# First batch rearranged: k transposed from f32, the DFT's sums and residual in PSUM, a written order of work, and new turns for the later stages

## The chip, the core and the metric

The kernel runs on one core of one Trainium2 chip. A core has a matrix engine (PE, with its weight loads shown apart as PEld), a vector engine (DVE), a scalar engine (ACT), GpSimd (POOL) and a sync engine (SP) that here only issues DMAs. PE writes to PSUM, of which this kernel uses eight banks; all POOL operations here read and write SBUF. Times are device microseconds of one execution; the number that counts is the median of several.

## What is computed

Four batches, eight heads, 768 positions, 64 columns per head. First a decayed linear attention, then an FFT over the sequence and over the 512 model columns, of which the real part is kept, then a normalised feed-forward layer:

```python
for t in range(S):
    state = gamma * state + einsum('bhd,bhe->bhde', k[:, :, t], v[:, :, t])
    y[:, :, t] = scale * einsum('bhd,bhde->bhe', q[:, :, t], state)
x = y.transpose(0, 2, 1, 3).reshape(B, S, H * D)
u = x + real(fft(fft(x, axis=1), axis=2))
un = (u - mean(u)) / sqrt(var(u) + 1e-6)
out = u + maximum(un @ w_ch1, 0.0) @ w_ch2        # 512 -> 2048 -> 512
```

## The kernel before

**Attention.** The sequence is cut into six chunks of 128 rows and the heads into four pairs. For each pair: q, k, v are loaded in f32 (`load_unit`, 384 KB each, on SP), cast to f16 on POOL (`q0_unit`, `k0_unit`, which scales k by a decay per row, `v0_unit`). PE transposes q and k with an identity (`t0_unit`, line 433), ACT copies the results out (`te_unit`, lines 441 and 444). PE forms the scores of each chunk (`am_unit`, wkA, line 458), DVE masks and scales them into atm (`ae_unit`, line 465). PE forms k'v of each chunk (`kv0_unit`, wkK, line 480), and one DVE scan runs the state through the chunks (`sc_unit`, line 489). The output y is atm v plus q times the state (`yi_unit`, `yx_unit`, lines 504 and 520); ACT scales it into x (`x0_unit`, line 533). Heads 4 to 7 lie mirrored in the second half of x. Pairs come in the order 0, 1, 3, 2.

**DFT.** Symmetry halves it twice. DVE folds x over the sequence (`fold_s`, tile xab, line 673), then over the columns (`fold_d`, tile eo, line 683). PE multiplies by cosine and sine tables (`s1_unit`, ps, line 730), ACT and DVE copy the result out as g (lines 737 and 739). The edge columns go a way of their own (`g0_a`, `g0_b`, `g0_c`). The second DFT (`s2_unit`, psum pq, lines 843 and 847) gives 128 rows of the mixed result: its two parts P and Q are joined by an ACT copy qn (line 855) and two DVE operations into u (lines 856 and 858). In the first batch's rows 0 to 383 (row blocks kb 0 to 2) half of x is put into pq first (`px_unit`), the mean comes from x (`xmean_unit`, `mean_unit`), and `norm_unit` writes un = mean - u (line 879); elsewhere POOL adds x (lines 864 and 866) and DVE takes the statistics. PE transposes un (`unT_unit`, line 914).

**Feed-forward.** `h_unit` and, for the first three row blocks, `h0_unit` (psh, lines 930 and 947) form relu(un w1), evicted by ACT or DVE into ht16; `ch_unit` (psc, line 973) multiplies by w2, DVE adds u, SP stores. The weights are cast while they are loaded, by eight DMAs on POOL's queue (`w1_unit`, `w2_unit`, lines 987 and 994).

**Order.** The engines run their instructions in program order. For the first batch the order is a hand-written list in `first_units`, and `pin` makes each engine keep it. Fillers, matmuls of zeros into a PSUM tile that nobody reads (`filler`, line 145), stand between its steps. All after that is a set of streams: each stream is a list of units with a start and an end in units of one batch's feed-forward work, `emit` sorts all units by that due time, and the attention and DFT of batch b + 1 so come to lie between the feed-forward matmuls ("majors") of batch b. The loads of the second batch wait for the seventh weight DMA and for a feed-forward matmul. From the third batch on, q, k and un are transposed by DMAs on SP.

**PSUM.** Five banks (ps_g) go round; two more (ps_y) and one for fillers (ps_w) serve the first batch alone and are given back, and three (ps_pm) for the feed-forward products take their place.

Of the kernel before, what the change touches and what calls it, by code (L numbers as in the profile page):

```python
# [18 lines left out]
P = 128  # L19
# [12 lines left out]
FB = 1  # L32
NPE = 2
ACT_ROWS = ((2, 5, 6, 7, 8, 9, 10, 14), (0, 3, 6, 7, 9, 10, 11, 12, 14, 15), (2, 4, 5, 6, 7, 8, 10, 14))
# [3 lines left out]
def kernel(  # L38
# [32 lines left out]
    first = ExitStack()  # L71
    ps_y = first.enter_context(tc.tile_pool(name="ps_y", bufs=2, space=PSUM))
    ps_w = first.enter_context(tc.tile_pool(name="ps_w", bufs=1, space=PSUM))
    ps_pm = None
# [65 lines left out]
    wps = ps_w.tile([P, DM], f32, tag="w", name="wps")  # L140

    def filler(n):
        def run():
            for _ in range(n):
                nc.tensor.matmul(wps, wz[:, 0:P], wz, start=True, stop=True)  # L145
        return run
# [5 lines left out]
    def load_unit(b, i, after=None):  # L152
        def run():
            h0 = 2 * PAIR_ORDER[i]
            for name, src in srcs.items():
# [3 lines left out]
                dma = nc.sync.dma_start(t, src[b, h0:h0 + 2].rearrange(rows, p=P))  # L159
# [21 lines left out]
    gexp = const.tile([P, 2, H], f32, tag="gexp")  # L181
    gq8, gkd = gexp[:, 0], gexp[:, 1]
    ident16 = const.tile([P, P], f16, tag="ident16")
    tmp = up.tile([P, NCH, DM], f32, tag="u32", name="tmp")
# [3 lines left out]
    rs = [tmp[:, 2 + n] if n < 4 else tmp2[:, n - 4] for n in range(10)]  # L188
    icoln = const.tile([P, 5], f32, tag="icoln")
# [8 lines left out]
    for h in range(H):  # L198
# [6 lines left out]
                            op0=ALU.mult)  # L205
    nc.scalar.activation(gexp, gexp, AF.Exp, bias=0.0, scale=1.0)
# [4 lines left out]
    make_identity(nc, ident16)  # L211
    nc.gpsimd.affine_select(out=maskf, in_=maskf, compare_op=ALU.is_ge, fill=0.0, base=0,
# [15 lines left out]

    def late_consts():
        with tc.issue_after(lb[0]["una"].ins):  # L230
            for h in range(H):
                nc.scalar.activation(maskp[:, h // 2, h % 2], maskf, AF.Copy, bias=0.0,
                                     scale=float(gam[h] ** (-P)))
# [59 lines left out]
    def csn_unit(c):  # L293
        def run():
            nc.scalar.activation(csn[:, c, :], rs[2 * c + 1][:, 0:384], AF.Sin, bias=hpi,
                                 scale=-float(2.0 * np.pi / S))
        return run
# [46 lines left out]
    def half_ids():  # L344
        nc.gpsimd.tensor_scalar(out=hid, in0=ident16, scalar1=0.5, scalar2=1.0, op0=ALU.mult,
                                op1=ALU.mult)
        nc.gpsimd.tensor_scalar(out=nhid, in0=ident16, scalar1=-0.5, scalar2=1.0, op0=ALU.mult,
                                op1=ALU.mult)

# [3 lines left out]
    at, q16_of, kd_of, v16_of, last_cast = {}, {}, {}, {}, {}  # L353
# [42 lines left out]
    def k0_unit(i):  # L396
        def run():
            h0 = 2 * PAIR_ORDER[i]
            k32 = in_of.pop(("k", 0, i))
            kd = kd_of[0, i] = kp.tile([P, NCH, 2, D], f16, tag="kd16", name="kd16")  # L400
            nc.gpsimd.tensor_scalar(out=kd[:, :, 0, :], in0=k32[:, 0], scalar1=gkd[:, h0:h0 + 1],
                                    scalar2=1.0, op0=ALU.mult, op1=ALU.mult)
            if i < 3:
                nc.gpsimd.tensor_scalar(out=kd[:, :, 1, :], in0=k32[:, 1],
                                        scalar1=gkd[:, h0 + 1:h0 + 2], scalar2=1.0,
                                        op0=ALU.mult, op1=ALU.mult)
            else:
                nc.scalar.activation(kd[:, :, 1, :], k32[:, 1], AF.Copy, bias=0.0,
                                     scale=gkd[:, h0 + 1:h0 + 2])
        return run  # L410

    def v0_unit(i):
        def run():
            v32 = in_of.pop(("v", 0, i)).rearrange("p h c d -> p c h d")
            v16 = v16_of[0, i] = vp.tile([P, NCH, 2, D], f16, tag="v16", name="v16")
            n = NCH if i < 3 else 3
            last_cast[0, i] = nc.gpsimd.tensor_scalar(
                out=v16[:, 0:n], in0=v32[:, 0:n], scalar1=1.0, scalar2=1.0, op0=ALU.mult,
                op1=ALU.mult)
            if n < NCH:  # L420
                nc.vector.tensor_copy(v16[:, n:], v32[:, n:])
        return run

    def t0_unit(i, part):
        def run():
            if part == 0:
                at[0, i] = dict(kT=tp.tile([P, NCH, P], f16, tag="kT", name="kT"),
                                qT=qts[i % 2][:, 0])
            src = (q16_of, kd_of)[part][0, i]
            tq = at[0, i]["tq", part] = ps_g.tile([P, NCH, P], f16, tag="g", name="tq",  # L430
                                                  padded_shape=[P, 8, P])
            for c in range(NCH):
                nc.tensor.transpose(tq[:, c, :], src[:, c].rearrange("p a b -> p (a b)"), ident16)
        return run

    def te_unit(i, part):
        def run():
            st = at[0, i]
            tq = st["tq", part]
            if part == 0:  # L440
                nc.scalar.copy(st["qT"].rearrange("p c t -> p (c t)").rearrange(
                    "p (t c) -> p t c", c=NCH), tq.rearrange("p c t -> p t c"))
            else:
                nc.scalar.copy(st["kT"], tq)
        return run

    def am_unit(i, half):
        def run():
            st = at[0, i]
            if half == 0:  # L450
                st["atm"] = ap_.tile([P, NCH, 2, P], f16, tag="atm", name="atm")
# [10 lines left out]
    def ae_unit(i, half, h2):  # L462
        def run():
# [3 lines left out]
                scalar=float(gam[2 * PAIR_ORDER[i] + h2] ** (-P)),  # L467
                in1=maskf.unsqueeze(1).to_broadcast([P, 3, P]), op0=ALU.mult, op1=ALU.mult)
        return run
# [25 lines left out]
    def yi_unit(i, h2):  # L495
        def run():
            st = at[0, i]
            first = i < 3
            if first:
                st["y", h2] = ps_y.tile([P, NCH, D], f32, tag="y", name="wkY",  # L500
                                        padded_shape=[P, 8, D])
# [7 lines left out]
    def yx_unit(i):  # L509
        def run():  # L510
            st = at[0, i]
            first = i == 3
            if first:
                for h2 in range(2):
                    st["y", h2] = ps_y.tile([P, NCH, D], f32, tag="y", name="wkY",
# [9 lines left out]
    def x0_unit(i, h2):  # L525
        def run():
# [6 lines left out]
            nc.scalar.activation(dst, at[0, i]["y", h2], AF.Copy, bias=0.0, scale=gq8[:, h:h + 1])  # L533
# [30 lines left out]
    def a0_unit(b, i, half):  # L564
        def run():
            st = at[b, i]
            hp = PAIR_ORDER[i]
            if half == 0:
# [93 lines left out]
    def fold_s(b, lo, hi, s0, s1):  # L662
        def run():
# [8 lines left out]
            for a, op in ((0, ALU.add), (1, ALU.subtract)):  # L672
# [32 lines left out]
    def xmean_unit(kb):  # L705
        def run():
            if kb == 0:
                fd[0]["xm"] = stt.tile([P, 4], f32, tag="xm", name="xm")
                fd[0]["mu"] = stt.tile([P, 4], f32, tag="mu", name="mu")
            junk = up.tile([P, 2, 257], f16, tag="un16", name="junk")  # L710
# [4 lines left out]
    def mean_unit(kb):  # L715
        def run():
            nc.vector.scalar_tensor_tensor(out=fd[0]["mu"][:, kb:kb + 1],
                                           in0=fd[0]["xm"][:, kb:kb + 1], scalar=1.0 / DM,
                                           in1=fd[0]["g0"][:, kb:kb + 1], op0=ALU.mult,
                                           op1=ALU.add)  # L720
        return run

    def s1_unit(b, e, cb):
        def run():
            eo, g, gr = fd[b]["eo"], fd[b]["g"], fd[b]["gr"]
            tab = csp if e == 0 else ssp
            ps = ps_g.tile([P, 2, NK], f32, tag="g", name="ps1", padded_shape=[P, 2, 256])
            for par in range(2):
                for sb in range(3):
# [5 lines left out]
            dst = g[:, gi].rearrange("p (i t) -> p t i", t=2)  # L735
            if e == 0 or ON_ACT["g"][min(b, 2)]:
                nc.scalar.copy(dst, ps)
            else:
                nc.vector.tensor_copy(dst, ps)
            if b:  # L740
                (nc.scalar.copy if ON_ACT["gr"][min(b, 2)] else nc.vector.tensor_copy)(
# [26 lines left out]
    def g0_b(b):  # L768
        xg = fd[b]["xg"]
        ps = fd[b]["ps0"] = ps_g.tile([P, 3, 4], f32, tag="g", name="ps0", padded_shape=[P, 3, 160])  # L770
# [17 lines left out]
    def px_unit(kb):  # L788
        def run():
            lb.setdefault(0, {})  # L790
            pq = lb[0]["pq", kb] = (ps_y if kb < 2 else ps_g).tile(
                [P, DM], f32, tag="y" if kb < 2 else "g", name="pq0")
            x = xts[0][:, kb]
            for n, (dst, half, side, lo, hi) in enumerate((
                    (pq[:, 0:257], hid, 0, 1, 258), (pq[:, 0:257], hid, 1, 1, 258),
                    (pq[:, 257:512], hid, 0, 2, 257), (pq[:, 257:512], nhid, 1, 2, 257))):
                nc.tensor.matmul(dst, half, x[:, side, lo:hi], start=(n == 0), stop=False,
                                 skip_group_check=True)
        return run

    def edge_zeros():
        for t in qns:
            nc.gpsimd.memset(t[:, 0:257:256], 0.0)

    def s2_unit(b, kb):
        def run():
            if kb == 0:
                pq0 = lb.get(b, {})
# [3 lines left out]
                lb[b].update(pq0)  # L812
# [6 lines left out]
            early = b == 0 and kb < 3  # L819
            pq = lb[0]["pq", kb] if early else ps_g.tile([P, DM], f32, tag="g", name="pq")  # L820
# [357 lines left out]
```

## Time and profile before

| what | value |
|---|---|
| median of 6 runs | 247.82 us (247.54 to 248.06) |
| the profiled execution | 247.79 us |
| its span | 246.0 us |
| instructions | 5309 |
| HBM read, written | 27.26 MB, 6.29 MB |
| first feed-forward matmul (psh) | starts 35.14 us |
| first second-layer matmul (psc) | starts 48.50 us |
| last matmul group | 235.71 us, for 7.11 us |
| DVE, ACT busy from 0 to 35 us | 30.92 us, 27.18 us |
| last v of the first batch | issued 15.05 us, lands 7.6 us later |

The span runs from the first to the last instruction of the profiled execution; 1.8 us of the execution lie outside it. A row of a group reads: line, engine, operation, output <- inputs, shape, count | busy time, mean duration of one | idle time before, and what ended it. Matmuls are pipelined, so a group's sum of durations is more than the time that it takes.

### The profile page before, as it was taken

What the parts mean: (1) busy time and instruction counts of PE and PEld (TensorE: products, weight loads), DVE (VectorE), ACT (ScalarE), POOL (GpSimd) and SP (SyncE); (2) the same over time, 40 slices, a digit from 0 to 9 for tenths busy, and PEclk for the clock granted to TensorE, in tenths of its full rate; (3) what the DMA queues carried; (4) which work ended last, traced back from release to release, by engine and by line L of the source; (5) the groups of instructions that cost most, each with busy time, mean ns of one, the idle gap of its engine ahead of it and who ended that gap; (6) DMA issues with size and microseconds to landing.
All of it is one profiled execution on the core that took longest, in us unless ns stands there. A gap on an engine that the chain in (4) does not pass through costs nothing.

```text
span 246.0 us, 5309 instructions
## 1 busy us (share of the span) xinstructions
PE 233.4 (95%) x2024; PEld 143.9 (59%) x2024; DVE 177.3 (72%) x430; ACT 124.3 (51%) x276; POOL 81.6 (33%) x146
## 2 busy tenths in 40 slices
PE   6797899999999999999999999999999998999994
PEld 2354668956676655665567446665666455445543
DVE  8997957898788788995987648887895657424112
ACT  8798669477785445742247415732257217202500
POOL 6667600485500068690001637660003214000000
PEclk9999999999999999999999999999999999999999
DMA  7998999799999287997999686596100231121012
GB/s 168 253 263 140 204 199 203 170 247 264 273 229 220 47 171 177 181 174 136 250 272 197 138 181 183 108 136 153 58 0 3 60 133 30 38 85 43 0 45 85
DMA packets 99209, 36.39 MB, mean 148 GB/s; under 512 B 89840, under 2 KB 96240, under 8 KB 99184
## 3 DMA queue, kind: packets, MB, share of 16 engines
q1 hardware_dynamic: 94960, 31.86, 61.5%
q0 software_dynamic: 4224, 4.19, 10.5%
q8 instruction: 16, 0.26, 0.5%
q14 instruction: 9, 0.07, 0.1%
HBM read 27.26 MB, written 6.29 MB: 136 GB/s over the span
## 4 chain that ended last, share of the span: by engine, by line
PE 67%; POOL 9%; DVE 8%; SPq 5%; DMA 4%; ACT 3%; issue 3%; POOLq 0%; DVEq 0%
PE psc L973 26%; PE psh L930 22%; SPq L159 3%; PE ps L730 3%; PE psh L947 3%; PE wkA L594 3%; DMA k<-in_k_dram 2%; PE wkY L648 2%; POOL u L864 2%; POOL u L866 2%; PE wkY L644 1%; DVE bst L883 1%; POOL kd L377 1%; DMA v<-in_v_dram 1%; DVE u L834 1%
## 5 line engine op out<-in xcount | busy, mean ns | idle before, releaser
L973 PE MATMUL psc<-w,ht 128*128 128x512 f16 (+1 forms) x400 | 89.6, 370 | 0.1
L930 PE MATMUL psh<-unT,w 128*128 128x384 f16 x448 | 81.3, 326 | 0.6 <-ACT ht L934 0.6
L973 PEld LDWEIGHTS <-ht 128*128 128x128 f16 x400 | 38.1, 98 | 35.5 <-issue 0.3
L930 PEld LDWEIGHTS <-w 128*128 128x128 f16 x448 | 42.3, 98 | 24.9 <-issue 1.3
L934 ACT ACTIVATE ht<-psh 128x384 f16<-128x384 f32 x64 | 30.7, 489 | 39.3 <-PE psh L930 38.3
L864 POOL TENSOR_TENSOR u<-u,x 128x256 f32<-128x256 f32 x21 | 13.4, 636 | 102.5 <-DVE u L834 89.7
L977 DVE SCALAR_TENSOR_TENSOR ob<-psc,stats,u 128x512 f32<-128x512 f32 (+1 forms) x25 | 18.0, 721 | 27.3 <-PE psc L973 27.2
L936 DVE TENSOR_SCALAR ht<-psh 128x384 f16<-128x384 f32 x48 | 26.3, 549 | 8.6 <-PE psh L930 8.3
L597 DVE TENSOR_TENSOR atm<-wkA,maskp 128x512 f16<-128x512 f32 x36 | 23.9, 681 | 1.0 <-PE wkA L594 1.0
L885 ACT ACTIVATE un<-u,stats 128x512 f16<-128x512 f32 x21 | 15.1, 721 | 17.1 <-DVE stats L884 8.8
L883 DVE BATCH_NORM_STATS2 bst<-u 128x6 f32<-128x512 f32 x21 | 14.6, 694 | 9.8 <-POOL u L866 9.7
L623 DVE SCALAR_TENSOR_TENSOR s<-s,gk,wkK 128x128 f16<-128x128 f16 x48 | 16.4, 341 | 2.4 <-ACT s L619 1.4
L656 ACT ACTIVATE x<-wkY,gexp 128x384 f16<-128x384 f32 x24 | 12.8, 582 | 9.3 <-PE wkY L648 9.3
L145 PE MATMUL wps<-ht 128*128 128x512 f16 x40 | 12.6, 418 | 2.1 <-POOL ht L196 2.1
L377 POOL TENSOR_SCALAR kd<-k,gexp 128x384 f16<-128x384 f32 x24 | 13.9, 591 | 1.7 <-DMA k<-in_k_dram 1.7
L866 POOL TENSOR_TENSOR u<-u,x 128x256 f32<-128x256 f32 x21 | 13.4, 636 | 2.8 <-DVE u L858 1.3
L594 PE MATMUL wkA<-qTz,kT 128*128 128x256 f16 x72 | 13.6, 273 | 0.0
L829 ACT COPY qn<-pq 128x128 f32<-128x128 f32 x18 | 5.0, 275 | 14.1 <-PE pq L827 13.9
L947 PE MATMUL psh<-unT,w 128*128 128x128 f16 x192 | 11.5, 219 | 0.1
L947 PEld LDWEIGHTS <-w 128*128 128x128 f16 x192 | 11.0, 98 | 0.7 <-issue 0.5
L382 POOL TENSOR_SCALAR v<-v 128x768 f16<-128x768 f32 x12 | 10.0, 834 | 2.4 <-DMA v<-in_v_dram 2.4
L594 PEld LDWEIGHTS <-kT 128*128 128x128 f16 x72 | 6.9, 98 | 6.0 <-DVE s L623 0.4
(164 smaller groups left out, 317.2 us busy)
## 6 DMA issues: line engine op xcount, KB each, us to landing
q<-in_q_dram SPq DMA_DIRECT2D x16, 384.0 KB, 6.1
k<-in_k_dram SPq DMA_DIRECT2D x16, 384.0 KB, 5.7
v<-in_v_dram SPq DMA_DIRECT2D x16, 384.0 KB, 6.6
out_dram<-ob SPq DMA_DIRECT2D x23, 256.0 KB, 2.6
w<-in_moe_w_ch_dram POOLq DMA_DIRECT2D x8, 512.0 KB, 11.2
out_dram<-ob SPq DMA_DIRECT2D x2, 128.0 KB, 1.7
unT<-un SPq DMA_TRANSPOSE x15, 2.4
qTz<-q16z SPq DMA_TRANSPOSE x8, 3.8
```

The lines of the kernel that those rows point to most:

```text
L594: mm = nc.tensor.matmul(wk[:, c2], st["kT"][:, c, :], st["qT"][:, :, c, :], start=True, stop=True)
L597: nc.vector.tensor_tensor(out=st["atm"][:, 2 * part:2 * part + 2], in0=wk, in1=maskp[:, PAIR_ORDER[i]].unsqueeze(1).to_broadcast([P, 2, 2, ...
L623: nc.vector.scalar_tensor_tensor(out=s16[:, c], in0=s16[:, c - 1], scalar=gk2[:, hp:hp + 1], in1=wk[:, c - c0], op0=ALU.mult, op1=ALU.add)
L864: nc.gpsimd.tensor_tensor(out=u[:, kb, 0:256], in0=u[:, kb, 0:256], in1=x[:, kb, 0, 1:257], op=ALU.add)
L866: nc.gpsimd.tensor_tensor(out=u[:, kb, 256:512], in0=u[:, kb, 256:512], in1=x[:, kb, 1, 257:1:-1], op=ALU.add)
L883: nc.vector.bn_stats(bst, u[:, kb, :])
L930: nc.tensor.matmul(psh, w116[:, cb, fb * P:(fb + 1) * P], unT[:, cb, rt * 384:(rt + 1) * 384], start=(cb == 0), stop=(cb == 3))
L934: nc.scalar.activation(ht16[:, fb, :], psh, AF.Relu, bias=0.0, scale=-1.0)
L936: nc.vector.tensor_scalar(out=ht16[:, fb, :], in0=psh, scalar1=-1.0, scalar2=0.0, op0=ALU.mult, op1=ALU.max)
L947: mm = nc.tensor.matmul(psh[:, f], w116[:, cb, fb * P:(fb + 1) * P], unT[:, cb, kb * P:(kb + 1) * P], start=(cb == 0), stop=(cb == 3))
L973: nc.tensor.matmul(psc[:, c0:c1], ht16[:, fb, rb3 * P:(rb3 + 1) * P], w216[:, fb, c0:c1], start=(fb == 0), stop=(fb == NFB - 1))
L977: nc.vector.scalar_tensor_tensor(out=ob[:, c0:c1], in0=psc[:, c0:c1], scalar=lb[b]["st"][:, rb, 3:4], in1=lb[b]["u"][:, rb, c0:c1], op0=AL ...
```

## The change

It rewrites the first batch and re-times the rest. What it computes is the same. By parts:

- `load_unit`: the first batch's k is loaded in two DMAs, one per head, laid out so that a chunk of both heads is contiguous.
- `tk_unit`, `ek_unit` in place of half of `t0_unit`, `te_unit`: PE transposes k32, the f32 as loaded, with an f32 identity, in two halves of three chunks, and ACT copies each half to kT in f16. The decay that the cast of k put on kT is now a column `gks`, used as scalar where atm is masked. POOL's cast of k remains for k'v.
- One of the sixteen maskings goes by ACT (a scaled copy) and POOL (the mask); v of the last pair is cast by POOL alone; one x of the last pair is written by DVE.
- `csn_unit` copies from the cosine table in place of three sines.
- `fold_d` is left out for the first batch: `s1_unit` adds both column halves in PSUM, for the odd part with a negated sine table (`neg_unit`, three POOL operations). Each sum comes in a part L (heads of pairs 0 and 1) and a part R (pairs 3 and 2).
- Row block 0: x enters PSUM through the identity, unhalved; `p2_unit` sums both parts there, for the upper half with reversed tables (`sr_unit`); un is formed straight from PSUM in two halves (`pn_unit`), on ACT and DVE, and u is written later (`pu_unit`). Row blocks 1 and 2 keep qn and u, in units of their own.
- `h0_unit` is split into its matmuls and its eviction.
- PSUM: ps_pm has its three banks from the start and serves y, the fillers, the edge columns and row block 0. Fillers count 128 columns per unit and are fewer: 17 matmuls in place of 40.
- The order of the first batch is a list of names, `ORDER`, and reaches to the ninth of the twelve `h0_unit`s; the last four (22, 20, 12, 10) are the first majors. The weights' DMAs come as w1 groups 2, 0, 3, 1 and w2 groups 1, 2, 0, 3. `late_consts` (eight maskp copies on ACT) is a stream of its own.
- The streams' times: some of `DM0`, `TS0`, `DA0`, `DA1`, `LD0`, `LD1`, `TS1` and `HT0` differ.

```diff
+ORDER = """
+f24_90 ts0 q0 ts2 ta02 ta00 tq0 f8_91 tka0 eq0 ts1 tkb0 eka0 f2_4 gk3 f2_10 f1_2 v0 ekb0 ta20
...
+ta30 a20 x10 f1_5 q3 kv2 a21 m200 ta32 ta40 pn2 m210 ta01 tq3 ka3 yi20 m201 x11 w12 sc2 eq3 m211
+ta31 kb3 tka3 tkb3 eka3 fsl yi21 yx2 ekb3 a30 cn0 a31 m300 v3 tL0 ac301 m311 x21 w10 kv3 m310
+x20 sL1 sc3 pm301 ta42 tL1 sr1 ta41 fs0 yx3 w13 yi31 yi30 tR0 vx31 w11 x30 sL0 g0a xm0 fs1 w21
+sR0 xm2 g0b sR1 w22 ae00 g0c ve10 tR1 af01 w20 px0 vf11 s20 w23 mean2 mean0 px2 an00 vn01 xm1
+px1 gr1 ut0 mean1 s21 xe1 au00 vu01 aq1 s22 u0 h00 aq2 u1 h02 gr3 am1 u2 h03 e00 am2 ut1 h01 e02
+vu1 e03 ut2 h13 e01 au2 h11 e13 gr2 h21 e11 h23 e21 gr0 e23
+""".split()
...
+                if b == 0 and name == "k":
+                    for h2 in range(2):
+                        dma = nc.sync.dma_start(t[:, :, h2], flat[:, h2])
...
+    def tk_unit(i, half):
+        def run():
+            k32 = in_of["k", 0, i]
+            tk = at[0, i]["tk", half] = ps_g.tile([P, 3, P], f32, tag="g", name="tk",
+                                                  padded_shape=[P, 4, P])
+            for c3 in range(3):
+                nc.tensor.transpose(tk[:, c3, :], k32[:, 3 * half + c3].rearrange(
+                    "p a b -> p (a b)"), ident32)
+    def ek_unit(i, half):
+            nc.scalar.copy(st["kT"][:, 3 * half:3 * half + 3], st["tk", half])
...
-                scalar=float(gam[2 * PAIR_ORDER[i] + h2] ** (-P)),
+                scalar=gks[:, 2 * PAIR_ORDER[i] + h2:2 * PAIR_ORDER[i] + h2 + 1],
...
+                for n in range(6 if direct else 0):
+                    i0, n = 2 + P * cb, 2 * (n % 3) + n // 3
+                    if part is None or n % 2 == part:
+                        nc.tensor.matmul(ps[:, par, :],
+                                         fd[b]["ab"][:, par, n // 2, n % 2, i0:i0 + P],
+                                         tab[:, par, n // 2, :], start=par == 0 and n == 0,
+                                         stop=n == 5, skip_group_check=True)
...
+            for n in sides:
+                nc.tensor.matmul(pq[n], ident16, xts[0][:, kb, n, slice(257, 1, -1) if n else
+                                                        slice(1, 257)],
+                                 start=True, stop=False, skip_group_check=True)
...
+    def pn_unit(kb, n, dve):
+            if dve:
+                nc.vector.tensor_scalar(out=dst, in0=pq[n], scalar1=-1.0,
+                                        scalar2=fd[0]["mu"][:, kb:kb + 1], op0=ALU.mult,
+                                        op1=ALU.add)
+            else:
+                nc.scalar.activation(dst, pq[n], AF.Identity, bias=fd[0]["mu"][:, kb:kb + 1],
+                                     scale=-1.0)
```

In `ORDER` the letters name units: q, ka, kb, v casts of a pair; tq, tk transposes and eq, ek their copies; a scores, m maskings; kv, sc, yi, yx, x as above (vx: x on DVE); fsl, fs0, fs1 folds; s and t cosine and sine sums with parts L and R; ae, af, ve, vf their evictions; px, s2, an, vn, ut, au, vu row blocks from pq to unT; h and e matmuls and evictions of `h0_unit`; w weights; f fillers; ta and ts tables.

The times of the streams, before and after:

```diff
-        dm = (0.12, 0.24, 0.3, 0.38) if b == 0 else (0.004, 0.140, 0.232, 0.341)
+DM0, DM1 = (0.130, 0.240, 0.297, 0.377), (0.004, 0.140, 0.232, 0.341)
-                ts = (0.249, 0.368, 0.410, 0.415, 0.507, 0.615, 0.680, 0.685)
+TS0 = (0.249, 0.368, 0.410, 0.415, 0.498, 0.570, 0.680, 0.685)
-                ts = [-0.040, -0.020] + [0.050 + 0.585 * sum(n[:j]) / sum(n)
+TS1 = (-0.040, 0.023, 0.050, 0.585)
-            da = (0.062, 0.080, 0.173, 0.203, 0.271, 0.321) if b == 0 else \
-                (0.063, 0.067, 0.048, 0.158, 0.168, 0.189)
+DA0, DA1 = (0.062, 0.080, 0.173, 0.203, 0.315, 0.321), (0.063, 0.067, 0.063, 0.158, 0.168, 0.189)
-                streams.append(([load_unit(1, i, 6) for i in range(4)], 0.180, 0.220))
-                streams.append(([load_unit(b + 1, i) for i in range(4)], b + -0.370, b + 0.075))
+LD0, LD1 = (0.172, 0.226), (-0.370, 0.235)
```

## Prediction

> **What bounds the kernel now.** I read the page first: its busy shares and the row of slices that shows the granted clock.
>
> ```profile
> PE 233.4 (95%) x2024; PEld 143.9 (59%) x2024; DVE 177.3 (72%) x430; ACT 124.3 (51%) x276; POOL 81.6 (33%) x146
> ...
> PEclk9999999999999999999999999999999999999999
> ```
>
> PE is the only engine near its limit, and its clock is full in every slice. Then the busy time of each engine by stretch (columns: length, then PE, PEld, DVE, ACT, POOL busy; clock; DMA share; GB/s):
>
> ```profile
> 0.00:35.00 35.00, 27.71 (x325) 16.15 (x326) 30.92 (x80) 27.18 (x57) 21.15 (x44) 1.00 1.10 205
> 35.00:50.00 15.00, 14.73 (x221) 12.97 (x219) 10.74 (x27) 10.63 (x30) 2.85 (x9) 1.00 1.05 189
> 50.00:100.00 50.00, 49.26 (x443) 30.96 (x442) 42.65 (x111) 31.57 (x64) 23.12 (x37) 1.00 0.97 204
> 100.00:150.00 50.00, 50.00 (x402) 30.45 (x400) 37.89 (x90) 21.48 (x51) 15.35 (x26) 1.00 0.98 191
> 150.00:200.00 50.00, 49.59 (x393) 29.81 (x392) 37.77 (x91) 21.66 (x51) 15.43 (x27) 1.00 0.39 87
> 200.00:243.00 43.00, 42.11 (x249) 23.59 (x246) 17.03 (x35) 11.75 (x28) 3.68 (x6) 1.00 0.16 50
> ```
>
> From 35 to 243 us PE idles 0.27 + 0.74 + 0 + 0.41 + 0.89 = 2.3 us. So the end is set by when the feed-forward stream starts, and then by PE's work; new turns in the later stages can win 2.3 us at the very most. Before 35 us PE is busy 27.7 us, and 12.6 us of the busy time in the page's L145 row is filler, whose results nobody reads. There the loads and then a chain of dependences set the pace. The timeline of PE gives the first feed-forward matmul:
>
> ```profile
> 35.14 3.00 PE L947 MATMUL psh<-unT,w 128*128 128x128 f16 x48
> ```
>
> The chain of waits, asked for the first 62 us, shows what is in front of it (start, us, what):
>
> ```profile
> 25.56 0.81 DVE s L489
> 26.37 0.91 DVE atm L465 x2
> 27.28 0.55 DVE xab L673 x2
> ...
> 27.86 0.57 DVE eo L683
> ...
> 29.60 1.69 PE ps L730 x18
> ...
> 31.31 0.59 DVE g L739
> ...
> 33.16 0.37 ACT qn L855
> 33.53 0.81 ACT un L879 x2
> ...
> 34.71 0.37 ACT unT L916
> ```
>
> The reader is to see a strict series: last state scan, masks, folds, DFT sums, evictions, second DFT, qn, u, un, transpose. The last v is issued on SP at 15.05 us and lands 7.6 us later, at 22.65; the 12.5 us from there to 35.14 are latency, not throughput.
>
> **The change, part by part.** Everything is counted up to the first feed-forward matmul, F, and then to the end.
>
> *k through f32 transposes.* 24 f16 transposes of the cast k and four 0.80 us copies (L444) go; 24 f32 transposes and eight half copies come. The POOL cast leaves the way to kT and stays on the way to the state. No f32 transpose is in this trace. Low bound: six f16 ones follow each other in 0.34 us (5.18 to 5.52 in PE's timeline), 0.06 us each. High bound: four passes, each with its LDWEIGHTS of 98 ns unhidden, 4 x (0.098 + 0.057) = 0.62 us. I take 0.2 us, the row it is nearest to: four times the columns, a 128x512 matmul at 0.216 us (12 in 2.59 us on the chain from 48.66). The half copy goes by the 128x384 eviction L934, 0.49 us. The last k lands at 14.46 + 6.9 = 21.36. Six transposes 1.2 us, to 22.6; the copies stand behind the q copy and a sine, done at 23.4, against 23.35 + 0.80 = 24.15 before: 0.7 us earlier. But the way to the state is as before: v lands at 22.65, and POOL now casts all of it (0.83, done 23.6, 0.3 later than the split cast).
>
> *Pair 3 to x.* PE issues two score halves and six early DFT matmuls (6 x 0.083) first, and the sixth PSUM buffer needs the first mask: kv3 at 24.3, against 24.68. Scan behind three masks (3 x 0.49 from 23.8): 25.3 to 26.1, against 25.56 to 26.37. Then yx 0.53, yi 0.34, and x on ACT and DVE side by side: 27.7, against 27.27 + 1.06 = 28.33. Step: 0.6 us.
>
> *x to g.* The fold over d (L683, two on the path, 0.57 + 0.5) is gone, since PE sums both sides; its price is 24 matmuls more, 24 x 0.083 = 2.0 us of PE, all but six of them on pairs already done, in time that fillers held. The last fold waits for the g0 copies on DVE (0.36 + 0.47): 28.2 to 28.85. Only sR1 and tR1 remain, 12 x 0.083, to 30.05, then evictions 0.6 on two engines: 30.7. Before, g was complete at 31.31 + 0.59 = 31.9. Step total now 1.2 us.
>
> *g to F.* For the first row block x goes into the sum through an identity, and un is read from PSUM in two halves on ACT and DVE. Gone from the chain: qn 0.37, u 0.49 + 0.47. Two of eight second-stage matmuls wait for the last g: 31.15. un 0.46 (L879, half a row), 31.65. But PE has px2, px1 (0.44 each), the transposes 0.22, s21 and s22 (0.44 each) in front of F: 31.05 + 2.0 = 33.05; the unT copies end at 32.5 and hide behind that. F at 33.1 us, 2.0 us earlier than 35.14. If POOL's negated tables (three, 0.30 to 0.59 each by L345 and L401) or the extra mask on POOL (0.64 by L864) come late, tR0 or yi30 waits; both have over 1 us in hand.
>
> *F to the first second-layer matmul.* It took 48.50 - 35.14 = 13.36 us before, for 12 x 0.89 + 2 x 0.22 + 6 x 0.22 = 12.4 us of work. The eight maskp copies (1.69 us of ACT at 38.92, before the first relu at 40.51) now come later. I take 12.8: 0.5 us more, 2.5 so far.
>
> *Costed at nothing:* four more k issues on SP (0.47 each, at worst 0.5 us once; SP waits for ring space, its last issue ends at 16.5 and nothing else needs it until 44.95); a column as scalar in the masks; PSUM pools merged to three shared buffers; csn as copies instead of sines. Fillers fall from 40 to 17 (20480 to 6400 columns, about 5.9 us of PE), which pays for the f32 transposes: 24 x 0.2 = 4.8. If the cover is gone, PE has none left per pair.
>
> *The later turns.* Most orders differ by a few matmuls. The loads of the third batch's last pair fall behind two transposing DMAs on SP (issues of 3.31 and 2.08 us), where out stores and unT transposes queue too. Between +2 and -2.3; I take -0.2.
>
> Sum: 2.5 + 0.2 = 2.7 us off a span of 246.0 whose run took 247.79 (the 1.8 around it stays); that run is at the median of 247.82. Forecast 245.1.
>
> *A rule against it.* The clock row above is full although transposes and fillers alternate. The Trainium skill (TensorE: Matmul & The Clock Gate, Part 4) states that PE-mode transposes don't count as busy for the clock gate, and that an idle window of about 3.4 us halves the clock. By the rule fewer fillers and more transposes would cost up to 1.7 us for one window at half clock (247); by the row I add nothing, since no gap of PE there grows past 2 us. The same skill (FP8 and Floating Point Precision, TensorE Precision Notes) gives true FP32 four passes, which speaks for the upper bound of the transposes.
>
> **Rivals.**
> 1. *f32 transposes at the high bound, PE the front's limit.* Six take 3.7 us; with q transposes 0.35, scores 0.42, kv 0.40, yi 0.34, yx 0.45 a pair needs 5.7 us of PE against the loads' 4.7. It decides from about 0.46 us each. Four pairs run 4 x 1.0 us late, F at 37.1, with 12.8 us more the second layer starts at 49.9 to 50.9 instead of 48.5: about 249.8. Against it: the 0.216 row.
> 2. *The weights hide the gain.* w transfers are issued from POOL from 20.57 us and landed 5.5 to 18.0 us later, some 2.5 us apart once queued: the fourth at 34.8. Now the second waits for the v cast, the third for the mask on POOL, so the fourth lands at about 35.3 and the last near 45. F at 33.1 needs the fourth at 35.9. That is in time by half a microsecond; half a transfer later, the front keeps about 1.2 us: 246.5.
> 3. *The later stream gives it back.* The second batch's loads wait for the seventh w transfer and a feed-forward matmul; they start at 43.5 instead of 44.95 while PE is 2.5 us ahead, and their 18.6 us are DMA time. PE then waits 1 us for casts, and the moved loads of the third batch 1 us more: 247.7, no change, and slower from there on.
>
> **How the numbers follow.** Forecast 0.62 (own range 243.8 to 246.2, from transposes of 0.06 to 0.3 and later turns of -1 to +0.5); rival 2, 0.18; rival 3, 0.10, half of it past no change; rival 1, 0.08; nothing of this 0.02. Runs of this kernel differ by about 0.2% (247.54 to 248.06), so 0.5 us is what can be told. Faster: forecast, rival 2 and a little of rival 3, 0.82; same 0.07; slower 0.11. Range 243.3 to 247.4: below it the later turns' whole 2.3, above it rival 1 and most of rival 3.
>
> **What would show it.** Right: first h matmul near 33.1, mean f32 transpose spacing under 0.3 us, no fold-over-d row for the first batch, L-part DFT matmuls before the last x, clock row full. Wrong: kT copies that PE ends late (rival 1), the first h waits ended by DMA w (2), waits on POOL casts near 50 to 65 or 95 to 110 us (3), or a 7 among the clock's first slices.

## The result, and the profile after

The changed kernel takes 248.40 us (median of 21 runs, 247.66 to 249.61), the kernel before 247.71 us on the same chips (42 runs, 247.41 to 248.29): a ratio of 1.003, 95% interval 1.0022 to 1.0039. It is slower by 0.7 us, where 2.7 us less were forecast. Its profiled run took 248.41 us with a span of 246.6 us; before it was 247.79 and 246.0.

The page of the changed kernel first, the busy shares and the clock:

```profile
PE 231.4 (94%) x2027; PEld 147.3 (60%) x2027; DVE 178.4 (72%) x428; ACT 122.4 (50%) x277; POOL 84.1 (34%) x150
...
PEclk9979999999999999999999999999999999999999
```

PE is busy for 2 us less than before, and is not done earlier. One slice of the clock is a 7. Busy time by stretch (columns as in the prediction: length; PE, PEld, DVE, ACT, POOL; clock; DMA share; GB/s), the second answer for 15 to 20 us alone:

```profile
0.00:35.00 35.00, 27.29 (x346) 20.56 (x347) 31.34 (x79) 27.66 (x64) 23.93 (x52) 0.95 1.06 201
35.00:50.00 15.00, 15.00 (x215) 12.95 (x212) 11.95 (x28) 8.86 (x22) 3.66 (x6) 1.00 1.18 211
50.00:100.00 50.00, 48.71 (x445) 31.02 (x444) 43.24 (x114) 32.10 (x66) 22.86 (x37) 1.00 0.95 201
100.00:150.00 50.00, 48.55 (x389) 29.06 (x387) 36.43 (x85) 20.28 (x48) 14.23 (x25) 1.00 0.97 185
...
15.00:20.00 5.00, 5.00 (x78) 3.96 (x76) 4.93 (x10) 3.54 (x8) 3.79 (x7) 0.66 1.17 251
```

From 100 to 150 us PE was busy for all of 50.00 us before; now it idles 1.45 us there. PE's timeline says where (start, duration, and in brackets the idle time in front and what ended it):

```profile
34.01 2.84 PE L1149 MATMUL psh<-unT,w 128*128 128x128 f16 x48
...
46.49 3.62 PE L1180 MATMUL psc<-w,ht 128*128 128x512 f16 x16
...
108.76 0.44 PE L694 MATMUL wkK<-v,kd 128*128 128x128 f16 x5 [0.61 <-ACT x L737]
113.27 0.39 PE L675 MATMUL wkA<-qTz,kT 128*128 128x256 f16 x2 [0.84 <-DMA kT<-kd]
```

The front did get shorter: the first psh starts 1.1 us earlier than before, the first second-layer matmul (psc) 2.0 us earlier. Since every kernel here issues the same 400 psc matmuls, the start of the n-th of them, compared with the kernel before, shows where a lead goes. From the traces (us; minus is earlier; "mended" is an experiment below):

| psc number | before, at | changed | mended | delayed front |
|---|---|---|---|---|
| 0 | 48.50 | -2.01 | -1.62 | +0.64 |
| 48 | 79.62 | -1.30 | -0.92 | +1.32 |
| 96 | 108.53 | -1.41 | -1.01 | +1.22 |
| 112 | 113.12 | +0.38 | -1.01 | +3.14 |
| 256 | 192.30 | +0.29 | -1.10 | +3.25 |
| 399, the last | 242.54 | +0.07 | -1.32 | +3.03 |
| end of the span | 245.97 | +0.67 | -0.71 | +3.59 |

Three losses are to be explained: 0.7 us between 48 and 80 us, 1.8 us between 108 and 113 us, and 0.6 us after the last matmul. (Between the numbers listed, the order of other work differs, so that only these rows compare the same work.)

The chain of waits of the changed kernel runs, at 113 us, through a transposing DMA:

```profile
106.34 0.96 POOL q16z L412 x2
107.30 0.72 POOL kd L415 x2
108.02 5.20 DMA kT<-kd
113.22 0.05 issue
113.27 0.39 PE wkA L675 x2
```

And so the place to look is SP's queue, which gives out loads, stores and transposing DMAs one after the other. Before:

```profile
87.28 0.39 SPq L159 DMA_DIRECT2D v<-in_v_dram  x1
87.75 0.79 SPq L159 DMA_DIRECT2D q<-in_q_dram  x1
...
93.15 1.51 SPq L542 DMA_TRANSPOSE qTz<-q16z  x1
94.76 1.56 SPq L544 DMA_TRANSPOSE kT<-kd  x1
...
98.87 3.31 SPq L542 DMA_TRANSPOSE qTz<-q16z  x1
...
104.47 2.53 SPq L910 DMA_TRANSPOSE unT<-un  x2
107.10 1.44 SPq L542 DMA_TRANSPOSE qTz<-q16z  x1
```

After:

```profile
85.72 0.39 SPq L193 DMA_DIRECT2D v<-in_v_dram  x1
...
91.65 1.54 SPq L623 DMA_TRANSPOSE qTz<-q16z  x1
93.30 1.55 SPq L625 DMA_TRANSPOSE kT<-kd  x1
94.91 0.57 SPq L193 DMA_DIRECT2D q<-in_q_dram  x1
...
97.27 3.52 SPq L623 DMA_TRANSPOSE qTz<-q16z  x1
...
102.54 0.57 SPq L193 DMA_DIRECT2D v<-in_v_dram  x1
103.21 3.17 SPq L1096 DMA_TRANSPOSE unT<-un  x2
106.48 1.45 SPq L623 DMA_TRANSPOSE qTz<-q16z  x1
```

Before, the last q load of the third batch goes out at 87.75, while SP has nothing else to do until 92. After, it stands behind the first two transposes, and the last v load among the later ones. The transposes start 1.5 us earlier than before (91.65 against 93.15), and by the third qTz only 0.6 us are left of it.

The two waits have different causes. The first, 0.61 us at 108.76, ends with an ACT eviction that stands behind un, and un waits for the transposing DMAs that were issued behind the v load at 102.54. Those rows of ACT:

```profile
107.42 0.72 ACT L1074 ACTIVATE un<-u,stats 128x512 f16<-128x512 f32 x1 [2.94 <-DMA unT<-un]
108.05 0.57 ACT L737 ACTIVATE x<-wkY,gexp 128x384 f16<-128x384 f32 x1
```

The second, 0.84 us at 113.27, is for the third pair's kT, which lands 5.20 us after its issue; before, it is 3.14. What the DMA engines move in that time (40 equal slices from issue to landing), and the one packet of 16 KB of instructions, on queue q8, that passes meanwhile:

```profile
GB/s 224 221 205 205 205 209 219 221 215 187 207 253 201 205 215 195 189 51 12 193 272 8 221 195 189 209 195 58 0 0 0 0 4 6 10 10 10 10 16 2
...
q8 instruction: 1, 0.02, 1.5%
```

For the last 1.6 us almost nothing moves. In the kernel before, the third kT has no such packet in its time:

```profile
GB/s 205 212 205 202 111 46 20 10 49 264 290 287 290 290 297 280 284 280 261 277 203 186 228 241 209 196 222 215 202 225 199 203 86 17 0 0 7 46 179 202
```

All eighteen traces agree. In twelve no packet of q8 passes while the third kT is under way, and it lands after 3.1 to 3.5 us; in six one does (the changed kernel, e1, e3, e4, e7, e9 below), it lands after 4.6 to 5.2 us, and only in these six PE waits for it. No run moves the packet alone, so that it holds the transfer up is likely, and not shown; the order on SP moves the transfer relative to it.

### The profile page after: what moved, and what is told of

Its sections match the earlier page's. It is cut to its first block, busy times and chain, and to the rows that moved or that the text cites. A ratio compares the mean times of both kernels' runs of the same rounds, so it can differ in the third digit from the quotient of the medians.

```text
span 246.6 us, 5329 instructions
## 1 busy us (share of the span) xinstructions
PE 231.4 (94%) x2027; PEld 147.3 (60%) x2027; DVE 178.4 (72%) x428; ACT 122.4 (50%) x277; POOL 84.1 (34%) x150
## 3 DMA queue, kind: packets, MB, share of 16 engines
HBM read 27.26 MB, written 6.29 MB: 136 GB/s over the span
## 4 chain that ended last, share of the span: by engine, by line
PE 63%; DVE 15%; POOL 9%; ACT 5%; DMA 4%; issue 3%; POOLq 0%; ACTq 0%
PE psc L1180 25%; PE psh L1130 20%; PE psh L1149 3%; POOL u L1061 3%; PE ps L841 3%; PE wkA L675 2%; DVE bst L1072 2%; DMA kT<-kd 2%; DVE atm L523 2%; POOL q16z L412 2%; POOL kd L415 2%; PE wkY L729 2%; DMA qTz<-q16z 2%; POOL u L1059 1%; PE wkY L725 1%
## 5 line engine op out<-in xcount | busy, mean ns | idle before, releaser
L737 ACT ACTIVATE x<-wkY,gexp 128x384 f16<-128x384 f32 x24 | 12.8, 582 | 8.7 <-PE wkY L729 8.7
L1038 DVE SCALAR_TENSOR_TENSOR u<-pq,g,qn 128x256 f32<-128x256 f32 x18 | 8.5, 473 | 3.3 <-PE psh L1130 2.5
```

## The experiments

All times are medians; ratios are to the kernel before, run beside it on the same chip, with 95% intervals. Waits and queues are from one profiled run of each kernel.

**1. All stream times put back** (e1), **and the new ones in the old kernel** (e2).

```diff
-DM0, DM1 = (0.130, 0.240, 0.297, 0.377), (0.004, 0.140, 0.232, 0.341)
+DM0, DM1 = (0.12, 0.24, 0.3, 0.38), (0.004, 0.140, 0.232, 0.341)
...
```

TS0, TS1, DA0, DA1, LD0 and LD1 are put back likewise; e2 has the reverse edit in the kernel before.

> The changed first batch, with every stream time (DM0, TS0, TS1, DA0, DA1, LD0, LD1) put back to the values of the kernel before. Theory T1 (the front's gain of 2.0 us at the first second-layer matmul is real, and the newly set turns of the later stages give it back): the time falls to 245.8 to 246.8 us, ratio 0.992 to 0.997 to the kernel before, and the matrix engine's waits at 107 to 113 us (0.6 and 0.8 us) are gone. Rival T2 (the later stages are held by loads and transposing DMAs that do not move with the front, whatever the turns): 247.9 to 248.8, the same as the changed kernel, with other waits in the place of these. Rival T3 (only the clock of the front matters): as T2.

Measured: 250.22 us, ratio 1.0108 (1.0077 to 1.0138), above every range given, with 2.1 us of waits for kT at 98 to 118 us. The theory that the new turns give the gain back falls: the old ones give back far more.

> The first batch of the kernel before, with the stream times of the changed kernel. T1: the turns alone cost what they cost in the changed kernel, 1.5 to 2.7 us, so 249.2 to 250.4 us, with waits of the matrix engine before wkK and wkA of the third batch. T2: nothing is given back where nothing was won, so 247.4 to 248.1. If the turns only fit together with the earlier front, something between or above: waits at other places than 107 to 113 us.

Measured: 247.60 us, 0.9996 (0.9985 to 1.0007). In the old kernel the new turns do nothing, and PE has no wait at 98 to 118 us. So this loss comes with the new first batch, under either set of turns.

**2. More filler** (e3), for the clock.

```diff
-... gk3 f2_10 f1_2 v0 ...  kb0 f3_6 ta10 ...  eka1 yi00 ...
+... gk3 f2_10 f24_2 v0 ... kb0 f12_6 ta10 ... eka1 f30_94 yi00 ...
```

> The changed kernel with more filler columns ahead of the three thin places of the matrix engine between 7 and 15 us (1 to 24, 3 to 12, 0 to 30 units of 128 columns, about 3.4 us of matmuls at full clock). T3 (the half clock from 16 to 19 us costs the front about 1 us, and its coming and going makes the wide spread of the times): the clock row is full, the first psh starts at 33.0 to 33.4 instead of 34.01, the runs lie within 0.7 us of each other instead of 2, and if the later stages let the gain through the time is 247.2 to 247.6. T1 and T2: the first psh may come earlier but the time stays 248.0 to 248.7, since the later waits take it back. If the fillers themselves stand in the way the first psh is later than 34.01.

Measured: 248.33 us, 1.0034 (1.0019 to 1.0049). In the profile the slow stretch moved to 20 to 25 us (clock 0.66) and the first psh came at 34.25. Three of the nine runs had a clock of 1.000 throughout; they took 248.23, 248.33 and 248.33 us. A full clock alone does not bring the end forward here, where PE waits 1.3 us at 98 to 118 us all the same.

**3. Only the loads and casts of the third batch put back** (e4).

```diff
-TS1 = (-0.040, 0.023, 0.050, 0.585)
+TS1 = (-0.040, -0.020, 0.050, 0.585)
-... LD1 = (0.172, 0.226), (-0.370, 0.235)
+... LD1 = (0.172, 0.226), (-0.370, 0.075)
```

> The changed kernel with two stream times put back only: the third and fourth batches' loads (LD1's end 0.235 to 0.075) and their first casts and transposes (TS1's second value 0.023 to -0.020). If the v and q loads behind the transposing DMAs on SP's queue are the whole of the later loss: the waits at 107 to 113 us go and the time is within 0.3 us of the run with all old turns, and 1 us or more below the changed kernel (247.4 or less). If the loss is in other turns (the stalls at 55 to 57 and at 91.7 us, 1.0 and 0.84 us): 247.8 to 248.5.

Measured: 248.59 us, 1.0044 (1.0024 to 1.0065). The v load is back in front of the second pair (97.65), the q load is not: it still stands at 95.42, behind the first two transposes, because the planner that orders the streams puts it there with either due time. PE waits 1.6 us for kT at 98 to 118: 0.86 for the second pair's, 0.78 for the third's. This is what showed the q load as the thing to move.

**4. A first try at moving it** (e5): an order edge holds the first qTz behind the q load, LD1's end at 0.075.

```diff
+    es.enter_context(tc.issue_after(ld_of["q", 2, 3].ins))
+    streams.append(([load_unit(2, 3, names="q")], b + 0.015, b + 0.015))
```

> The changed kernel with LD1's end back at 0.075 and the third batch's last q load held ahead of that batch's first transposing DMAs on SP's queue, where the kernel before has it (all kernels with the new first batch had it behind them). Theory W (the matrix engine's lead is stopped at 104 to 113 us by SP's queue, which gives out the third batch's loads and transposing DMAs one after the other; the last pair's three loads between them delay them): the waits at 104 to 113 us shrink from 1.8 us to under 0.8, time 247.0 to 247.8. Rival C (the chain of POOL casts and residual sums after the second batch's DFT decides, whatever SP issues): 248.1 to 248.8, as the changed kernel.

Measured: 248.48 us, 1.0035 (1.002 to 1.005), and 1.0 us of waits, now for the second pair's kT. The edit missed its aim: a store that waits for its result came to stand ahead of the load, and another behind it, so that q went out at 91.06, not in the gap, and the first qTz at 93.35 instead of 91.65. The time lies in the range of rival C, but as the load did not get its old place, the run does not decide for it.

**5. The last pair's loads left out**, in the changed kernel (e6) and in the kernel before (e6b).

```diff
+                if (b, i) == (2, 3):
+                    in_of[name, b, i] = kept[name]
+                    continue
```

> The changed kernel without the three loads of the third batch's last pair (1.15 MB); the casts read the pair before it again. W: SP's queue and its rings are free for the transposes, the waits at 104 to 113 us are gone, and the front's gain of some 1.4 us at 90 us reaches the end: 246.2 to 247.2. C: the same waits, 248.0 to 248.7. If only bytes in flight matter and not the queue, in between: 247.2 to 247.8.

Measured: 247.44 us, 0.9991 (0.998 to 1.0001), 1.0 us below the changed kernel, no wait at 98 to 116 us. That is above W's range, in the one given for bytes in flight alone; in its profile the lead was down to 0.41 us at psc 48 already, and none of it went between psc 96 and 112. The second qTz is issued in 1.42 us, against 3.52 behind the q and k loads in the changed kernel and 4.98 in e5.

> The kernel before without the same three loads, as the control. It has no wait of the matrix engine at 104 to 113 us, so by W and by C it gains nothing there: 247.4 to 247.9. If it gains as much as the changed kernel does (1 us or more), the loads cost everywhere and the wall is not particular to the earlier front.

Measured: 247.71 us, 0.9996 (0.9987 to 1.0005): nothing to be told. In this kernel, where they stand, the loads cost nothing.

**6. The front held back by filler** (e7).

```diff
-... s22 u0 h00 ...
+... s22 u0 f37_95 h00 ...
```

> The changed kernel with 37 units of filler (4736 columns, 2.0 us at full clock) directly ahead of the first feed-forward matmul. W: the lead is lost at the wall anyway, so two microseconds more of delay cost little: 248.2 to 249.2, with the waits at 104 to 113 us shorter by what the delay took. C or a front that counts in full: 249.9 to 250.5, the waits unchanged.

Measured: 251.32 us, 1.0139 (1.0125 to 1.0153). Theory W falls in its strong form: there is no fixed time at which the lead is stopped. Against the changed kernel's profile the first psc comes 2.65 us later and the last one 2.96 us, with 1.58 us of waits there, against 1.45; the third kT again has a q8 packet in its time and lands after 5.0 us. The chain from the second batch's second DFT over POOL's sums and casts and SP's transposes moves with PE, so the front counts in full, and the extra length of the chain is paid again.

**7. SP's order made that of the kernel before** (e8, "mended").

```diff
-TS1 = (-0.040, 0.023, 0.050, 0.585)
+TS1 = (-0.040, -0.020, 0.050, 0.585)
-... LD1 = (0.172, 0.226), (-0.370, 0.235)
+... LD1 = (0.172, 0.226), (-0.450, 0.030)
+    streams.append(([load_unit(2, 3, names="q")], b + -0.08, b + -0.08))
+    es.enter_context(tc.issue_after(ld_of["q", 2, 3].ins))
+    es.enter_context(tc.issue_after(at[2, 0]["td"].ins))
```

The last two edges hold the first batch's store of row block 4 behind the q load, and that of row block 5 behind the first kT; the first qTz stays behind the q load as in e5.

> The changed kernel with the order on SP's queue from 80 to 113 us made that of the kernel before (v load, q load, store, two transposes of the first pair, store, k load, v load, second pair), by order edges and by LD1 = (-0.45, 0.03) and TS1's second value -0.020; the q load then goes out in the gap before the first transposes. Theory W2 (the later loss is this q load and its followers among the transposing DMAs, whose issue a load ahead of them stretches from 1.42 to 3.3 to 5.0 us; the front itself counts in full): the waits at 103 to 113 us fall from 1.8 us to under 0.4, and 1.3 to 1.6 us of the front's gain reach the end: 246.5 to 247.3. If another thing of the new first batch makes the chain from the second DFT to the transposes longer: 247.8 to 248.6 with a wait of 1 us or more left at 103 to 113.

Measured: 246.95 us (246.54 to 247.21), 0.9972 (0.9961 to 0.9982), faster than both kernels. SP's queue of this kernel:

```profile
86.12 0.39 SPq L195 DMA_DIRECT2D v<-in_v_dram  x1
86.60 0.78 SPq L195 DMA_DIRECT2D q<-in_q_dram  x1
...
92.03 1.54 SPq L629 DMA_TRANSPOSE qTz<-q16z  x1
...
103.18 2.51 SPq L1102 DMA_TRANSPOSE unT<-un  x2
105.79 1.46 SPq L629 DMA_TRANSPOSE qTz<-q16z  x1
```

The q load is in the gap again, un's transposes take 2.51 us instead of 3.17, the third qTz comes 1.3 us earlier than before, and PE does not wait at 98 to 116 us. The lead of 1.0 us at psc 96 is still there at 112. Both waits are gone: un's transposes stand behind no load, and the third kT, issued 0.7 us earlier than in the changed kernel, has landed at 110.4, before the q8 packet at 111.0. That the order costs the 1.8 us is shown; how much of it goes by the packet is not.

**8. The same, with the filler of e3** (e9), **and with DM0, TS0, DA0, DA1 and LD0 of the kernel before** (e10).

> The same with the additional fillers of e3 at 7 to 15 us. In e3 three runs with the clock at 1.000 had 248.2 to 248.3 us, where others had 248.2 to 249.8 at 0.992 to 0.998. W2: the time is that of e8 within 0.3 us, with fewer runs 1 us above it. T3 (the front's clock): 0.5 to 1.0 us below e8.

Measured: 247.15 us, 0.9987 (0.9976 to 0.9998). In its profile the clock is full and the first psc 2.25 us ahead; 0.7 us of it went between psc 96 and 112, where PE waits for the third kT until 111.94. It has a q8 packet in its time and lands after 4.60 us, though SP's order is the mended one. So this run does not show what a full clock is worth at the end.

> As e8, and the other stream times (DM0, TS0, DA0, DA1, LD0) of the kernel before. The run with all old turns had 250.2 us, 1.8 more than the changed kernel, and its order on SP's queue was wrong in the same place. W2: with the order mended, old and new turns are within 0.5 us of each other, 246.5 to 247.6. If the new turns are worth something of their own beside it (the wait of 1.3 us at 80 and 74 us in the old ones): 1 us above e8 or more.

Measured: 247.77 us, 1.0009 (0.9999 to 1.0019). With the order mended the old turns come out 2.5 us below e1, and stay 0.8 us behind e8, between the two ranges given: the new turns are worth about that much in the new kernel.

**9. The one load moved in the kernel before** (e11).

```diff
+                    if (b, i, name) == (2, 3, "q"):
+                        es.enter_context(tc.issue_after(at[2, 0]["td"].ins))
```

> The kernel before with one thing moved: the third batch's last q load stands behind that batch's first two transposing DMAs on SP's queue, as in the changed kernel. W2: the second pair's transposes come 1 to 2 us later and PE waits for them at 100 to 113 us: 248.5 to 249.8. If the place of this load is not what costs: 247.6 to 248.1.

Measured: 248.50 us, 1.0041 (1.0027 to 1.0054), 0.9 us more for one load moved by 8.5 us. Its queue, and PE's only wait at 98 to 116 us:

```profile
96.21 0.57 SPq L162 DMA_DIRECT2D q<-in_q_dram  x1
...
98.06 1.78 SPq L162 DMA_DIRECT2D v<-in_v_dram  x1
100.43 4.12 SPq L545 DMA_TRANSPOSE qTz<-q16z  x1
```

```profile
107.46 0.39 PE L597 MATMUL wkA<-qTz,kT 128*128 128x256 f16 x2 [0.88 <-DMA kT<-kd]
```

The loads behind it are late too, the second qTz takes 4.12 us instead of 3.31, and the second pair's kT comes late. No q8 packet passes in that kT's time, so here the load's place makes a wait without one. It is not the wait of the changed kernel, which was for un's transposes and the third kT.

**10. The end of the program.** From the end of the last store's issue to the end of the span it is 2.9 us in the changed kernel (246.64 - 243.76) and in e8, but 2.3 in the kernel before (245.97 - 243.70). Among the DMA queues of the last microseconds (kind, packets, MB, share) the changed kernel has two packets of instructions,

```profile
q14 instruction: 2, 0.02, 0.3%
```

and the kernel before one. The edits: six one-column memsets on POOL (e12) or copies on ACT (e13) in the last batch of the kernel before, of a tile nobody reads; and three q casts of the fourth batch moved from POOL to ACT in the mended kernel (e14).

> The kernel before with six more POOL instructions (one-column memsets of a tile nobody reads, in the last batch, where POOL idles). POOL's program is then as long as in the changed kernel. Theory P (the end of the program waits for one more fetch of POOL's instructions): the span from the last store's issue to the end is 2.8 instead of 2.3 us, with two instruction packets instead of one after the last store, the matrix engine's last group where it was (235.7), and the time 0.4 to 0.6 us up, 248.0 to 248.4. Otherwise: 2.3 us and 247.5 to 247.9.

Measured: 248.21 us, 1.0011 (1.0002 to 1.002), two instruction packets, 2.6 us (246.28 - 243.68), the last psc where it was.

> The control: the kernel before with six more ACT instructions at the same place (one-column copies). P: end as before, 2.3 us and 247.5 to 247.9. If it is the number of instructions on any engine: 2.8 us and 248.0 to 248.4.

Measured: 247.86 us, 1.0002 (0.9993 to 1.0011), one packet, 2.3 us. So POOL's longer program costs 0.3 of the 0.6 us; the other 0.3 stay open. That the end waits for the packets, as theory P has it, is not shown: they start after the span has ended (247.28 and 248.24 in the changed kernel), and e6 has one packet with 3.0 us.

> The mended kernel (e8) with the q casts of the fourth batch's pairs 2 to 4 on ACT, so that POOL's program is seven shorter and below that of the kernel before. P: the end takes 2.3 us instead of 2.8 and the time is 0.4 to 0.6 us below e8, 246.3 to 246.7. Otherwise: 246.7 to 247.2. If ACT is short of time at 140 to 190 us the matrix engine's last group comes later than in e8.

Measured: 247.42 us, 0.9985 (0.9967 to 1.0003), above both ranges, with one packet and 2.5 us at the end, 0.3 less than in e8. But PE waits 0.90 us for an ACT eviction at 155 us, which eats it up. Inconclusive as an improvement.

**11. The v load behind the second pair** (e15: e8, with the third batch's last v load due at 1.235).

> The mended kernel (e8) with the third batch's last v load behind the second pair's transposing DMAs. The q transpose's issue, 3.67 us behind the k and v loads in e8, falls to 1.5 to 2.2. The matrix engine does not wait there in e8's profile, so by W2 the median stays within 0.2 us of e8 (246.8 to 247.2). If the remaining loads still cost in most runs: 0.3 us or more below e8. If the v load now stretches the un transposes instead: 0.3 us or more above.

Measured: 247.13 us, 0.9979 (0.9963 to 0.9995), the second qTz in 2.04 us. No gain over e8 that can be told, as expected where PE does not wait.

## Why the prediction was wrong

**The f32 transposes** were priced at 0.2 us each, between 0.06 and 0.62. From the first six to the next instruction on PE it is 0.66 us (6.17 to 6.83), 0.11 us each at full clock; at half clock, three take 0.64 us (17.75 to 18.39), 0.21 each. Rival 1 did not come up. The four passes that the Trainium skill gives for true FP32 (FP8 and Floating Point Precision, TensorE Precision Notes) do not show as a fourfold time per transpose: a f16 one takes 0.06.

**F**, the first feed-forward matmul, was forecast at 33.1 us and came at 34.01. The step that failed in the front is "pair 3 to x": the state scan on DVE was put at 25.3 and runs at 26.45 to 27.26, behind three masks that start at 24.86 instead of 23.8, since a mask of the pair before and a fold of x keep DVE until 24.82; x is whole at 28.9 instead of 27.7. From x to g (2.8 us against 3.0) and from g to F (2.3 against 2.4) the sums held, and from F to the first psc it took 12.48 us against 12.8. DVE, at 4.76 to 4.93 us of every 5 from 5 to 20 us, was not in the sum as a queue. So the front won 2.0 us instead of 2.5.

**The clock.** "By the row I add nothing, since no gap of PE there grows past 2 us": the gaps did stay below that (after the first 2.1 us of the span, the longest is 1.82 us, ahead of 14.86), but PE was busy for only 2.93 and 2.48 us of the two stretches of 5 before 15 us, and from 16 to 19 us the granted clock was 0.50. The rule of the Trainium skill weighed there (TensorE: Matmul & The Clock Gate, Part 4 for the transposes, Part 1 for the idle window) forecast the clock better, though no gap here comes near its window of 3.4 us. Whether the transposes or the thin work did it, no run separates: in e3 PE was busy for 5.00, 4.53 and 4.13 us of the three stretches of 5 before 20 us, and the clock still fell at 21. What it costs the front: the two profiles of the new first batch with a full clock (e5, e9) have F at 33.74 and 33.76; those with a slower stretch at 34.01 to 34.95 (e7 left out), 0.3 to 1.2 us later. It varies between runs of one program (mean clock 0.979 to 0.993 in the changed kernel's), as the same page says of its free-running window (Part 1). Whether it reaches the end depends on what follows: in the changed kernel the runs with a mean clock below 0.988 and those of 0.990 or more have the same median (248.40 and 248.41 us), with SP's order mended they differ (e10: 248.12 and 247.36; e15: 247.64 and 247.09).

**The later turns** were the step that failed, and that decided. "The loads of the third batch's last pair fall behind two transposing DMAs on SP. Between +2 and -2.3; I take -0.2": a gain of 0.2 us was put where 1.8 us are lost. The place was right and the upper bound would have held it; the value was taken near the middle instead of following the queue. And the reason was in part wrong: the due times were blamed, while the planner's place for the q load comes with the new first batch (e1, e4) and the new times are worth 0.8 us (e10 against e8). Why the planner puts it there is not settled. The sum had no term for the slow landing of the third kT either.

**Rival 3** named one more thing that is seen: the second batch's loads start at 44.07 instead of 44.95 while PE is 2.0 us ahead, POOL's casts then wait for them, and 0.7 us of lead are gone by 80 us, near the 1 us it gave. The loads wait for a feed-forward matmul, and start 2.42 us ahead of the first psc instead of 3.55; in the delayed front of e7 it is 2.42 again, and 0.7 us go again. PE itself waits there 0.34 us for a state scan on DVE and 0.18 for an ACT copy of kT. That the loads are the cause was not tested by itself. **Rival 2** did not occur. Not in the sum at all: the 0.6 us at the end.

In sum, against the kernel before: -2.0 at the first psc, +0.7 to 80 us, -0.1 to 108, +1.8 to 113, -0.3 to the last psc, +0.6 at the end: +0.7 in the spans and in the medians.

## What to carry to other kernels

Where a planner fixes the order, read the order that it made for every queue after a change, also far behind the edit: loads that had filled a gap, and now stood among transposing DMAs, took back 1.8 of the 2.0 us that the rearranged front had won; in the kernel before, one load of 384 KB moved so cost 0.9 us. A stall that stays when the front is delayed (e7) is not tied to a fixed time; look for what was put into the chain that ends in it. Leaving a suspected transfer out (e6), and moving it in the kernel that has no stall (e11), tells place from cost in two runs. And look at a transfer's landing as well as at its issue: over half of the wait at 108 to 113 us was for a landing.

## What the runs showed of the hardware

- A transposing DMA issued behind loads is stretched on its issuing queue: the second pair's qTz took 1.42 us with no load in the four microseconds ahead (e6; 1.43 in e6b), 1.75 and 2.04 behind one (e2, e15), and 3.0 to 5.0 behind two or three (all others).
- A transposing DMA with a 16 KB instruction packet of queue q8 in its time landed late: the third kT after 4.6 to 5.2 us in the six traces with one, after 3.1 to 3.5 in the twelve without.
- The clock fell to half for 3.4 us without any gap of PE over 1.82 us, after 10 us in which PE was busy for about half of the time; in e5 a profile of nearly the same front (3.55 and 2.65 us busy of 5) kept it full. In other profiles of the new front it stayed at half for 6.8 us (e8) or 10.2 us (e10), two and three times as long.
- Six more POOL instructions of no work put 0.3 us on the end, after the last store; six ACT instructions did not.
